# Windowed attention and a feed-forward layer in float32: chunk 0's second to fourth pair of heads in split form, and a PSUM bank for each head's values

## The chip, the cores and the metric

One core of a Trainium2 chip runs the whole program. The metric is the time of one execution on the device, in microseconds (us). The kernel before took 1069.58 us, the median of three runs (1069.06 to 1069.76). One further execution was taken with the hardware profiler; every row of a trace in this text is from such a profiled execution.

Engines are named as the profile does: PE is TensorE (matmul) and PEld its weight loads, DVE is VectorE, ACT is ScalarE, POOL is GpSimd, SP is SyncE, which here only issues transfers.

## The reference

The kernel computes attention over a causal window of 128 positions with a linear bias for each head, and then a two-layer feed-forward network:

```python
# q, k, v: (8, 8, 576, 64) float32
scores = scale * np.matmul(q, k.transpose(0, 1, 3, 2))
bias = slopes[:, None, None] * (-np.abs(rel))[None]       # slopes 2**-1 ... 2**-8
mask = (rel >= 0) & (rel < 128)                           # rel = row - column
scores = np.where(mask, scores + bias[None], -1e9)
attn = softmax(scores)
x = (attn @ v).transpose(0, 2, 1, 3).reshape(4608, 512)
h = x @ w_in                                              # (4608, 2048)
g = np.where(h >= 1, h, np.where(h <= -1, 0, (h + 1)**2 / 4))
out = g @ w_out                                           # (4608, 512)
```

The weights w_in and w_out arrive as float64 and are turned into float32 on the chip.

## The kernel before, in words

The 4608 tokens are cut into 12 chunks of 384 (three query blocks of 128). Within a chunk the 8 heads are taken as 4 pairs; pair p = 4c + g is pair g of chunk c, and m = 2p or 2p + 1 numbers its heads through the whole program. So heads 0 to 7 belong to chunk 0, and their pairs are 0 to 3. The feed-forward layer of a chunk needs the outputs of all its 8 heads: column block g of its input, `xn`, comes from pair g.

A head passes through these steps, each in a function of its own: `load_qk` and `load_v` start the transfers on the SP queue. `prepare_q`, `prepare_k` and `prepare_v` bring q, k and v into the form for TensorE. `scores` makes the scores (tile s), their biased maxima on DVE (line 249), the exponentials on ACT (line 251), the sum and its reciprocal (257, 258), and folds two neighbouring blocks into weights `ep` (262, 264). `weights_t` transposes `ep` (line 273, tile p), and ACT and POOL make from it the masked weights `lu`. `values` multiplies these with v (tile x) into `xn`.

There are two forms. In the **plain** form (chunks 0 and 1, `LIGHT = 2`) the operands stay in float32: one scale of q on ACT, nothing for k and v, one copy and two masks of 128x384 for `lu` (lines 276 to 279), float32 matmuls (lines 243 and 314). In the **split** form (all later chunks) each operand is a high and a low part in fp32r: q by two ACT and two DVE instructions (198, 199), k by a cast of both heads' rows and a subtraction (208, 209), v the same way (217, 218), `lu` by a cast, a subtraction and two masks of 128x768 (283 to 288), fp32r matmuls over high and low parts (245, 246, 338), and a sum of the parts for `xn` (339 to 342). For the split form the keys are loaded twice, once into each half of the partitions (lines 174 to 176).

The feed-forward layer of chunk c has 16 tiles fc of the hidden layer. `split_x` splits `xn` (xh on ACT, line 356, xl on DVE, line 357). `layer1` adds 12 fp32r matmuls into tile h (lines 363 to 365) and forms g; `layer2` follows two tiles behind and accumulates into three PSUM banks, `acc`. In chunk 0 it multiplies in float32 with `wf` (line 393), later in split form (lines 396 to 398). The weights of tile fc are fetched over the ACT queue and converted on ACT and DVE (lines 113 to 116, 135, 136), the first four in the opening of the program between the heads of chunk 0, the others beside chunk 0's own feed-forward layer.

PSUM has eight banks: three of `ps_acc` (tag acc), one for h, four that scores, transposes and values share (`bank`). In chunk 0 the two heads of a pair write the upper and lower half of one bank of `ps_acc`, and one copy of 128 rows takes both to `xn` (line 319, on ACT for g = 0 and 2, on DVE for g = 1 and 3).

SBUF tiles with one buffer set an order of their own: a tile of a tag can be written when the tile before it under this tag has been read for the last time. A plain pair with an odd number keeps k under the tag kk and v under the tag vs, tags that only the split form fills otherwise; so two plain pairs in a row have tiles of their own.

The order of each engine's instructions comes from a scheduler that moves them ahead of time by its own estimate; on the chip each engine works its list from front to back.

Of the kernel before, what the change touches and what calls it, by code (L numbers as in the profile page):

```python
# [18 lines left out]
def windowed_attention_then_ffn(  # L19
# [38 lines left out]
    NEG = -1.0e30  # L58

    LIGHT = 2  # L60
# [102 lines left out]
    def load_qk(p):  # L163

        c, g = divmod(p, NPAIR)
        n = CH + before(c) * P
        st = pair[p] = {}
        qr = st["qr"] = ap1.tile([P, CH], F32, name=f"qr_{p}", tag="qr")
        DMA.dma_start(qr, q[g * P:(g + 1) * P, c * CH:(c + 1) * CH])
        kr = st["kr"] = ap1.tile([P, 2, CH + P], F32, name=f"kr_{p}", tag="kk" if c < LIGHT and p % 2 else "kr")  # L170
        if c < LIGHT:
            DMA.dma_start(kr[:, 0, :n], k[g * P:(g + 1) * P, (c + 1) * CH - n:(c + 1) * CH])
            return
        for half in (slice(0, D), slice(D, P)):
            DMA.dma_start(kr[half, :, :n],
                          k[g * P:(g + 1) * P, (c + 1) * CH - n:(c + 1) * CH].rearrange("(j d) t -> d j t", j=2))

    def load_v(p):
        c, g = divmod(p, NPAIR)
        nb = NQB + before(c)  # L180
        if c < LIGHT and p % 2:
            t = ap1.tile([P, 2, NQB + 1, 2, D], F32, name=f"vn_{p}", tag="vs")[:, 0]
        else:
            t = ap1.tile([P, NQB + 1, 2, D], F32, name=f"vn_{p}", tag="vn")
        pair[p]["vn"] = t
        DMA.dma_start(t[:, :nb].rearrange("p i j d -> p i (j d)"),
                      v[(c + 1) * CH - nb * P:(c + 1) * CH, g * P:(g + 1) * P].rearrange("(i p) d -> p i d", p=P))

    def prepare_q(p):
        ql = pair[p]["ql"] = ap1.tile([P, 2, CH], F32R, name=f"ql_{p}", tag="ql")  # L190
        qr = pair[p]["qr"]
        if p // NPAIR < LIGHT:
# [8 lines left out]
    def prepare_k(p):  # L201
        if p // NPAIR < LIGHT:
# [8 lines left out]
    def prepare_v(p):  # L211
        if p // NPAIR < LIGHT:
# [7 lines left out]
    def scores(m, blks):  # L220
# [14 lines left out]
        for n, i in enumerate(blks):  # L235
# [5 lines left out]
            if c < LIGHT:  # L241
# [25 lines left out]
    def weights_t(m):  # L267
# [6 lines left out]
        if m < LIGHT * H:  # L274
# [17 lines left out]
    def values(m):  # L292
# [6 lines left out]
        if c == 0:  # L299

            if j == 0:
                pair[p]["px"] = ps_acc.tile([P, DM], F32, name=f"x_{m}", tag="acc")
            pb = pair[p]["px"]
        else:
            pb = bank(f"x_{m}")
        px, pf = pb[:, :CH], pb.rearrange("r (i w) -> r i w", w=P)
        o = xn[c, g][lo_rows[j]]
        if c < LIGHT:
            po = px[lo_rows[j]] if c == 0 else px[:D]
# [7 lines left out]
            if c == 0:  # L317
                if j:
                    (V.tensor_copy if g % 2 else S.copy)(xn[c, g], px)
            elif j:  # L320
# [205 lines left out]
```

## Time and profile before

| What | Value |
|---|---|
| Median of three runs | 1069.58 us |
| The profiled execution | 1071.97 us, its span 1070.3 us |
| Busy in the span: PE, PEld | 1034.4 us (97%), 900.9 us (84%) |
| Busy in the span: DVE, ACT, POOL | 790.2 us (74%), 619.1 us (58%), 370.6 us (35%) |
| Granted TensorE clock over the span | 0.99 |

A busy TensorE isn't TensorE at its peak: matmuls overlap, and their ends are modelled. So the share of 97% says little of a stretch; what one waits for there says more. A group of instructions has one row: line, engine, operation, out<-in, shape and count, then busy time and the mean of one in ns, then the idle time of the engine just ahead of them and what ended it. A row of the waits names the waiting engine, tile and line, then whom it waited for, then total, count and longest. The views by stage give the busy time of each engine in a stretch (with the number of instructions), the granted clock, the DMA share and GB/s.

### The profile page before, as it was taken

Reading aid. Unit: us, or ns where it says so; the run is one execution under the profiler, and the core shown is the slowest. Engines: PE = TensorE matmul, PEld = TensorE weight load, DVE = VectorE, ACT = ScalarE, POOL = GpSimd, SP = SyncE. Lnnn points to the kernel's source line nnn. Section 1 sums busy time; section 2 is a strip of 40 time slices with the busy share of each in tenths; the row PEclk is TensorE's granted clock in tenths of the full one; section 3 lists DMA queues with packets and bytes.
Section 4 is the critical chain, followed back from the end, with each engine's and each line's share of the span. In section 5 each row is a group of like instructions: output and inputs, shape, how many; then the busy total and the mean of one; then the engine's idle time right before and its main releaser. Section 6 shows DMA issues by size and latency. Waiting matters only on the chain.

```text
span 1070.3 us, 16779 instructions
## 1 busy us (share of the span) xinstructions
PE 1034.4 (97%) x5472; PEld 900.9 (84%) x5472; DVE 790.2 (74%) x2249; ACT 619.1 (58%) x1475; POOL 370.6 (35%) x419
## 2 busy tenths in 40 slices
PE   6899999999999999999999999999999999999998
PEld 3566667998988988998998989899899889899996
DVE  3687799888887688877678887767787897862322
ACT  4686876556655556556557556555565665742322
POOL 2121003334443343443343443443334444332221
PEclk9889999999999999999999999999999999999999
DMA  5455512121122122121211212111121221200000
GB/s 190 139 188 189 175 45 69 34 59 60 45 65 67 39 62 79 33 56 35 66 47 50 82 47 65 63 30 37 60 65 37 77 65 38 76 1 1 30 1 30
DMA packets 58903, 69.50 MB, mean 65 GB/s; under 512 B 4032, under 2 KB 44480, under 8 KB 58816
## 3 DMA queue, kind: packets, MB, share of 16 engines
q1 hardware_dynamic: 48064, 51.66, 16.8%
q10 hardware_dynamic: 10752, 16.78, 4.5%
q8 instruction: 43, 0.70, 0.3%
q14 instruction: 44, 0.36, 0.1%
HBM read 58.98 MB, written 9.44 MB: 64 GB/s over the span
## 4 chain that ended last, share of the span: by engine, by line
PE 82%; DVE 8%; ACT 5%; issue 2%; POOL 2%; DMA 0%; ACTq 0%; DVEq 0%; POOLq 0%
PE h L363 11%; PE h L364 11%; PE h L365 11%; PE acc L396 10%; PE acc L397 10%; PE acc L398 10%; PE x L338 5%; PE acc L393 3%; PE p L273 3%; PE s L246 2%; PE s L245 2%; PE x L314 2%; PE s L243 2%; ACT z L251 1%; POOL lu L288 1%
## 5 line engine op out<-in xcount | busy, mean ns | idle before, releaser
L382 POOL TENSOR_TENSOR gl<-g,gh 128x384 fp32r<-128x384 f32 x176 | 184.1, 1046 | 434.9 <-ACT gh L381 422.0
L363 PE MATMUL h<-xh,wi 128*128 128x384 f32 x768 | 265.0, 345 | 1.8 <-ACT sg L372 1.6
L364 PE MATMUL h<-xl,wi 128*128 128x384 f32 x768 | 260.3, 339 | 0.6 <-DVE xl L357 0.6
L365 PE MATMUL h<-xh,wi 128*128 128x384 f32 x768 | 259.4, 338 | 0.0
L396 PE MATMUL acc<-wo,gh 128*128 128x512 f32 x528 | 211.8, 401 | 8.1 <-ACT gh L381 8.1
L373 DVE SCALAR_TENSOR_TENSOR g<-sg 128x384 f32<-128x384 f32 x192 | 108.6, 565 | 150.4 <-ACT sg L372 139.0
L397 PE MATMUL acc<-wo,gh 128*128 128x512 f32 x528 | 207.8, 394 | 0.0
L381 ACT CAST gh<-g 128x384 fp32r<-128x384 f32 x176 | 90.4, 513 | 192.5 <-DVE g L374 182.1
L372 ACT ACTIVATE sg<-h,quarter 128x384 f32<-128x384 f32 x192 | 111.2, 579 | 141.4 <-PE h L365 140.6
L251 ACT ACTIVATE z<-z,nmax 128x256 f32<-128x256 f32 (+2 forms) x288 | 139.2, 486 | 33.8 <-DVE nmax L249 31.7
L398 PE MATMUL acc<-wo,gl 128*128 128x512 f32 x528 | 155.5, 398 | 0.0
L363 PEld LDWEIGHTS h<-xh,wi 128*128 128x128 f32 x768 | 144.5, 188 | 11.0 <-ACT sg L372 3.2
L364 PEld LDWEIGHTS h<-xl,wi 128*128 128x128 f32 x768 | 144.5, 188 | 7.2 <-issue 2.0
L365 PEld LDWEIGHTS h<-xh,wi 128*128 128x128 f32 x768 | 144.4, 188 | 0.0
L249 DVE CUSTOM_DVE_ANT_0 z<-s,rel 128x256 f32<-128x256 f32 (+2 forms) x256 | 94.3, 394 | 52.8 <-PE s L246 43.3
L264 DVE CUSTOM_DVE_ANT_0 ep<-z,rc 128x128 f32<-128x128 f32 x256 | 129.4, 546 | 1.5
L286 POOL TENSOR_SCALAR_AFFINE_SELECT lu<-lu 128x768 fp32r<-128x768 f32 x80 | 80.7, 1008 | 128.7 <-DVE lu L284 120.1
L396 PEld LDWEIGHTS acc<-wo,gh 128*128 128x128 f32 x528 | 99.4, 188 | 27.3 <-ACT gh L381 10.5
L374 DVE SCALAR_TENSOR_TENSOR g<-sg,g 128x384 f32<-128x384 f32 x192 | 111.9, 583 | 3.7
L398 PEld LDWEIGHTS acc<-wo,gl 128*128 128x128 f32 x528 | 97.0, 188 | 19.7 <-POOL gl L382 0.2
L397 PEld LDWEIGHTS acc<-wo,gh 128*128 128x128 f32 x528 | 99.4, 188 | 16.5
L288 POOL TENSOR_SCALAR_AFFINE_SELECT lu<-lu 128x768 fp32r<-128x768 f32 x80 | 81.3, 1017 | 4.6
(78 smaller groups left out, 1451.4 us busy)
## 6 DMA issues: line engine op xcount, KB each, us to landing
kr<-in_k_dram SPq DMA_DIRECT2D x60, 256.0 KB, 3.8
qr<-in_q_dram SPq DMA_DIRECT2D x48, 192.0 KB, 3.4
out_dram<-o SPq DMA_DIRECT2D x36, 256.0 KB, 2.3
rawi<-in_moe_w_in_dram ACTq DMA_DIRECT2D x16, 512.0 KB, 3.9
rawo<-in_moe_w_out_dram ACTq DMA_DIRECT2D x16, 512.0 KB, 5.0
vn<-in_v_dram SPq DMA_DIRECT2D x32, 256.0 KB, 2.7
kr<-in_k_dram SPq DMA_DIRECT2D x28, 192.0 KB, 3.2
vn<-in_v_dram SPq DMA_DIRECT2D x16, 192.0 KB, 2.5
```

The costliest lines, as they stand in the source:

```text
L251: S.activation(z[:, i, c0:], z[:, i, c0:], AF.Exp, bias=nmax[:, i:i + 1], scale=-1.0, accum_out=sm[:, i, 0:1])
L264: st["folded"] = V.tensor_tensor_reduce(out=ep[:, i, :], in0=z[:, i, :P], in1=z[:, i, P:], op0=ALU.add, op1=ALU.add, scale=rc[:, i:i + 1], ...
L363: T.matmul(ph, wi[fc][:, 0, cc, :], xh, start=(cc == 0), stop=False)
L364: T.matmul(ph, wi[fc][:, 0, cc, :], xl, start=False, stop=False)
L365: T.matmul(ph, wi[fc][:, 1, cc, :], xh, start=False, stop=(cc == NCC - 1))
L372: first = S.activation(sg, ph, AF.Relu, bias=quarter[:, 0:1], scale=0.25)
L373: V.scalar_tensor_tensor(g, sg, 0.5, sg, ALU.min, ALU.mult)
L374: last = V.scalar_tensor_tensor(g, sg, -0.25, g, ALU.add, ALU.max)
L382: G.tensor_tensor(gl, g, gh.bitcast(F32), ALU.subtract)
L396: T.matmul(a, gh[:, ts], wo[fc][:, 0], start=first, stop=False)
L397: T.matmul(a, gh[:, ts], wo[fc][:, 1], start=False, stop=False)
L398: T.matmul(a, gl[:, ts], wo[fc][:, 0], start=False, stop=last)
```

## The change

`LIGHT` goes. A function `plain(p)` says for each pair whether it is plain: pair 0, and the four pairs of chunk 1. Pairs 1 to 3 of chunk 0 are now in split form. In `values` every head of chunk 0 gets a bank of `ps_acc` for itself, and `xn` is filled head by head: for the two heads of pair 0 by a DVE and an ACT copy of 64 rows, for heads 2 to 7 by the sum of the split form.

```diff
-    LIGHT = 2
+    def plain(p):
+
+        return p == 0 or NPAIR <= p < 2 * NPAIR
...
-        kr = st["kr"] = ap1.tile([P, 2, CH + P], F32, name=f"kr_{p}", tag="kk" if c < LIGHT and p % 2 else "kr")
-        if c < LIGHT:
+        kr = st["kr"] = ap1.tile([P, 2, CH + P], F32, name=f"kr_{p}", tag="kk" if plain(p) and p % 2 else "kr")
+        if plain(p):
...
-        if c < LIGHT and p % 2:
+        if plain(p) and p % 2:
             t = ap1.tile([P, 2, NQB + 1, 2, D], F32, name=f"vn_{p}", tag="vs")[:, 0]
...
-        if m < LIGHT * H:
+        if plain(m // 2):
             own = lu[:, 0, 1::2, :].bitcast(F32)
...
-        if c == 0:
-
-            if j == 0:
-                pair[p]["px"] = ps_acc.tile([P, DM], F32, name=f"x_{m}", tag="acc")
-            pb = pair[p]["px"]
-        else:
-            pb = bank(f"x_{m}")
+
+        pb = ps_acc.tile([P, DM], F32, name=f"x_{m}", tag="acc") if c == 0 else bank(f"x_{m}")
         px, pf = pb[:, :CH], pb.rearrange("r (i w) -> r i w", w=P)
         o = xn[c, g][lo_rows[j]]
-        if c < LIGHT:
-            po = px[lo_rows[j]] if c == 0 else px[:D]
+        if plain(p):
+            po = px[:D]
...
-            if c == 0:
-                if j:
-                    (V.tensor_copy if g % 2 else S.copy)(xn[c, g], px)
-            elif j:
+            if j:
                 S.copy(o, po)
             else:
                 V.tensor_copy(o, po)
```

The same replacement of `c < LIGHT` by `plain(p)` stands in `prepare_q`, `prepare_k`, `prepare_v` and `scores`. Lines behind `plain` move by two, those behind `values` by minus six.

The scheduler puts the new instructions between the old ones. In the rows below a tile's name is followed by the number of its pair (kr, kk, kl, vn, vs, ql) or head (s, z, rc, ep, p, lu, x) and a running number.

On DVE, in the opening, from the maxima of head 3 to the sum of its exponentials; before:

```order
L249 ISA z_3_235,nmax_3_236<-s_3_2_244,rel_98 128x256
L249 ISA nmax_3_236 128x1
L115 TENSOR_SCALAR f_i0_221<-rawi0_125 128x512
L116 ISA f_i0_221<-rawi0_125,f_i0_221 128x1024
L257 TENSOR_REDUCE rc_3_248<-sums_108 128x3
L258 RECIPROCAL rc_3_248<-rc_3_248 128x3
L262 TENSOR_TENSOR ep_3_234<-z_3_235,rc_3_248 128x128
```

And after the change:

```order
L251 ISA z_3_248,nmax_3_249<-s_3_2_259,rel_98 128x256
L251 ISA nmax_3_249 128x1
L201 SCALAR_TENSOR_TENSOR ql_2_274<-qr_2_183,ql_2_274 64x384
L138 TENSOR_TENSOR wi0_238<-f_i0_233,wi0_238 128x512
L220 TENSOR_TENSOR vs_1_316<-vn_1_196,vs_1_316 128x6x64
L286 TENSOR_TENSOR lu_2_284<-p_2_285,lu_2_284 128x3x128
L117 TENSOR_SCALAR f_o0_294<-rawo0_128 128x512
L259 TENSOR_REDUCE rc_3_264<-sums_108 128x3
```

The low parts of pair 2's q, of pair 1's v and of head 2's weights stand ahead of head 3's sum. With heads 2, 4, 6 and 7 only one or two instructions stand at this place.

On SP, from the third transfer on, before:

```order
L186 DMA vn_0_117<-in_v_dram 128x3x128
L172 DMA kr_1_123<-in_k_dram 128x384
L169 DMA qr_1_121<-in_q_dram 128x384
L186 DMA vn_1_187<-in_v_dram 128x3x128
L172 DMA kr_2_177<-in_k_dram 128x384
L169 DMA qr_2_175<-in_q_dram 128x384
```

And after:

```order
L188 DMA vn_0_117<-in_v_dram 128x3x128
L171 DMA qr_1_121<-in_q_dram 128x384
L177 DMA kr_1_123<-in_k_dram 64x2x384 x2
L171 DMA qr_2_183<-in_q_dram 128x384
L177 DMA kr_2_185<-in_k_dram 64x2x384 x2
L188 DMA vn_1_196<-in_v_dram 128x3x128
L177 DMA kr_3_281<-in_k_dram 64x2x384 x2
```

The keys come in two transfers of half the partitions. Pair 1's v (vn_1) has moved behind the keys of pair 2, and its tile is now that of pair 0's v, which the values of head 1 read last.

On PE, from the end of the first hidden tile (h_0_0) on, before:

```order
L363 MATMUL h_0_0_600<-xh_0_3_596,wi0_226 128x384
L273 MATMUL p_9_571<-ident_82,ep_9_508 128x128
L364 MATMUL h_0_0_600<-xl_0_3_597,wi0_226 128x384
L365 MATMUL h_0_0_600<-xh_0_3_596,wi0_226 128x384
L314 MATMUL x_8_637<-lu_8_535,vn_4_454 64x256 x2
L314 MATMUL x_8_637<-lu_8_535,vn_4_454 64x128 x2
L243 MATMUL s_11_0_646<-kr_5_440,ql_5_529 128x256 x2
L243 MATMUL s_11_2_653<-kr_5_440,ql_5_529 128x192
L273 MATMUL p_10_707<-ident_82,ep_10_549 128x128 x3
L363 MATMUL h_0_1_664<-xh_0_0_584,wi1_283 128x384
```

And after:

```order
L357 MATMUL h_0_0_689<-xh_0_3_685,wi0_238 128x384
L275 MATMUL p_9_660<-ident_82,ep_9_592 128x128
L311 MATMUL x_8_726<-lu_8_619,vn_4_532 64x256 x2
L311 MATMUL x_8_726<-lu_8_619,vn_4_532 64x128 x2
L275 MATMUL p_9_660<-ident_82,ep_9_592 128x128 x2
L358 MATMUL h_0_0_689<-xl_0_3_686,wi0_238 128x384
L359 MATMUL h_0_0_689<-xh_0_3_685,wi0_238 128x384
L245 MATMUL s_11_0_735<-kr_5_509,ql_5_613 128x256 x2
L245 MATMUL s_11_2_742<-kr_5_509,ql_5_613 128x192
L275 MATMUL p_10_796<-ident_82,ep_10_638 128x128 x3
L311 MATMUL x_9_839<-lu_9_659,vn_4_532 64x256 x2
```

The values of head 8 have moved ahead of the end of the first hidden tile, and those of head 9 ahead of the second. From the fifth hidden tile of chunk 0 on the lists of PE are the same in both kernels, and those of the other engines from about there.

More of the change, by code (lines that the diff above doesn't have):

```diff
@@ L191, in prepare_q @@
         qr = pair[p]["qr"]
-        if p // NPAIR < LIGHT:
+        if plain(p):
             S.activation(ql[:, 0].bitcast(F32), qr, AF.Copy, scale=qscale[:, p % NPAIR:p % NPAIR + 1])
@@ L201, in prepare_k @@
     def prepare_k(p):
-        if p // NPAIR < LIGHT:
+        if plain(p):
             return
@@ L211, in prepare_v @@
     def prepare_v(p):
-        if p // NPAIR < LIGHT:
+        if plain(p):
             return
@@ L240, in scores @@
             win.append((o, c0, lone))
-            if c < LIGHT:
+            if plain(p):
                 r, qs, ks = lo_rows[j], slice(i * P, (i + 1) * P), slice(k0, k0 + 2 * P - c0)
@@ L298, in values @@
             xn[c, g] = xp1.tile([P, CH], F32, name=f"xn_{c}_{g}", tag=f"xn{g}")
-        if c == 0:
-            if j == 0:
-                pair[p]["px"] = ps_acc.tile([P, DM], F32, name=f"x_{m}", tag="acc")
-            pb = pair[p]["px"]
-        else:
-            pb = bank(f"x_{m}")
+        pb = ps_acc.tile([P, DM], F32, name=f"x_{m}", tag="acc") if c == 0 else bank(f"x_{m}")
         px, pf = pb[:, :CH], pb.rearrange("r (i w) -> r i w", w=P)
         o = xn[c, g][lo_rows[j]]
-        if c < LIGHT:
-            po = px[lo_rows[j]] if c == 0 else px[:D]
+        if plain(p):
+            po = px[:D]
             todo = [i for i in (0, 1, 2, -1) if i + b0 >= 0]
```

## The prediction

> **What bounds the kernel now.** I read the chain of waits first, then a table by stage of the stretch that it points to. In the chain the change can only touch the opening of the program; from the first accumulating matmul of the second layer (line 393) on, TensorE runs without a gap.
>
> ```profile
> 34.05 2.33 PE x L314 x6
> 36.38 2.43 PE s L243 x6
> 38.81 2.32 PE x L314 x6
> ...
> 44.97 1.30 PE x L314 x6
> ...
> 51.45 1.34 ACT z L251 x5
> 52.79 0.19 ACT z L251
> 53.01 0.17 DVE rc L257
> 53.20 0.19 DVE rc L258
> ...
> 62.36 2.75 PE x L314 x8
> 65.11 1.95 PE s L243 x6
> 67.07 0.48 PE p L273 x3
> 67.55 0.18 PE h L363
> ...
> 69.66 1.44 PE x L314 x8
> 71.11 0.63 PE acc L393
> ```
>
> The columns are start, duration, engine, tile, line. Two things are to be seen. The float32 score (s) and value (x) matmuls of chunk 0 lie on the chain, at 2.3 to 2.4 us a head in one place and 1.30 us in another, so TensorE's clock was not the same. And the last stretch, from 62.36 to 71.11, is a queue of TensorE alone.
>
> ```profile
> core 0: us, PE busy (x) PEld busy (x) DVE busy (x) ACT busy (x) POOL busy (x), PEclk, DMA share, GB/s
> 12.30:61.30 49.00, 43.20 (x139) 24.87 (x139) 30.90 (x139) 31.71 (x90) 10.21 (x21) 0.84 0.45 145
> 61.30:71.10 9.80, 9.80 (x42) 7.00 (x40) 8.54 (x30) 8.42 (x21) 2.43 (x5) 0.75 0.42 136
> ```
>
> I cut the opening where VectorE stands at the same work in both kernels: at 12.3 it has finished the maxima of head 1, and at 61.3 it has finished xl of the fourth column block (line 357), which the first hidden tile (fc 0) needs last. In those 49.0 us VectorE is busy 30.90 and idle 18.1. Its three largest waits tell why:
>
> ```profile
> DVE rc L257 <- ACT z L251: 10.4, 6, 4.3
> DVE z L249 <- PE s L243: 3.8, 3, 3.0
> DVE xn L319 <- PE x L314: 2.2, 2, 1.1
> ```
>
> 6.0 of it are waits for TensorE directly, 10.4 for the exponentials, which themselves were late behind TensorE in part. So the opening is paced by TensorE and by the round of one head (scores, maximum, exponential, fold, transpose, mask, values), with VectorE in reserve.
>
> **What the change takes from TensorE.** A plain head has 640 score columns and 640 value columns in float32. The split head has 1280 of each in fp32r. From a later chunk:
>
> ```profile
> 183.95 0.82 PE x L338 x7
> ```
>
> Seven split value matmuls take 0.82, five take 0.59, against 1.30 at full clock for the plain head; the scores, with as many columns, go the same way. That is about 1.4 us a head at full clock and 2.4 at half, for six heads 8.5 to 14.5 us of TensorE. If TensorE alone paced the opening, all of it would be won.
>
> **What it adds.** These rows give the mean of each added form over the whole kernel (after the bar: busy, mean ns):
>
> ```profile
> L199 DVE SCALAR_TENSOR_TENSOR ql<-qr,ql 64x384 fp32r<-64x384 f32 x80 | 59.3, 742 | 2.6 <-ACT ql L198 0.2
> L209 DVE TENSOR_TENSOR kl<-kr,kk 128x768 fp32r<-128x768 f32 x12 | 13.6, 1135 | 0.1
> L218 DVE TENSOR_TENSOR vs<-vn,vs 128x384 fp32r<-128x384 f32 x12 | 6.9, 573 | 0.0
> L284 DVE TENSOR_TENSOR lu<-p,lu 128x384 fp32r<-128x384 f32 x80 | 44.4, 555 | 4.6 <-ACT lu L283 3.3
> L340 DVE TENSOR_TENSOR xn<-x,xn 64x384 f32<-64x384 f32 x80 | 43.7, 546 | 4.1 <-ACT xn L339 2.9
> L342 DVE TENSOR_TENSOR xn<-x,xn 64x128 f32<-64x128 f32 x80 | 22.3, 279 | 1.8
> L319 DVE COPY xn<-x 128x384 f32<-128x384 f32 x2 | 1.1, 558 | 2.2 <-PE x L314 2.2
> ```
>
> A pair costs VectorE 2x0.742 (ql) + 1.135 (kl) + 0.573 (vs) + 2x0.555 (lu) + 2x0.546 + 2x0.279 (xn) = 5.95 us. Three pairs are 17.9. One of their old copies (g = 1) and that of g = 3 go, 2x0.558, and pair 0 gains a copy of 64 rows, taken as long as one of 128: together 17.3. The window has its own level for a form that both have:
>
> ```profile
> L264 DVE CUSTOM_DVE_ANT_0 ep<-z,rc 128x128 f32<-128x128 f32 x20 | 6.4, 363 | 0.1
> L264 DVE CUSTOM_DVE_ANT_0 ep<-z,rc 128x128 f32<-128x128 f32 x256 | 129.4, 546 | 1.5
> L286 POOL TENSOR_SCALAR_AFFINE_SELECT lu<-lu 128x768 fp32r<-128x768 f32 x80 | 80.7, 1008 | 128.7 <-DVE lu L284 120.1 <-DVE rc L257 8.5
> ```
>
> The fold takes 363 ns in the window and 546 in the whole kernel, a ratio of 0.66, so the lower bound of the added work is 0.66 x 17.3 = 11.4 us and the upper one 17.3. GpSimd's share explains the difference: 10.21 of 49.0 now; with twelve selects of 1.0 us in place of twelve of half that it comes to about 16 of 49, near the page's 35% for the whole kernel. I take 15.5, nearer to the upper end. The Trainium skill, "SBUF — State Buffer", on what shares the port pair, says that a VectorE instruction with two SBUF inputs and a GpSimd instruction that reads SBUF lock each other out; the rise from 363 to 546 agrees, and by that rule alone the sum would take the 17.3.
>
> ScalarE gains a kk and a vs cast, a second half of ql, and copies of 64 rows instead of 128:
>
> ```profile
> L193 ACT ACTIVATE ql<-qr,qscale 128x384 f32<-128x384 f32 x8 | 4.8, 604 | 1.1 <-PE s L243 1.1
> L198 ACT ACTIVATE ql<-qr 64x384 fp32r<-64x384 f32 x80 | 41.7, 521 | 1.0
> L208 ACT CAST kk<-kr 128x768 fp32r<-128x768 f32 x12 | 10.0, 836 | 1.6 <-PE s L245 1.4
> L217 ACT CAST vs<-vn 128x384 fp32r<-128x384 f32 x12 | 6.1, 512 | 1.6 <-PE x L338 1.6
> L339 ACT COPY xn<-x 64x384 f32<-64x384 f32 x80 | 38.1, 476 | 16.0 <-PE x L338 12.7 <-DVE xl L357 1.8
> ```
>
> With ql at 0.60 now and 2x0.52 then, a pair is 0.44 + 0.84 + 0.51 + about 0.7 = 2.5 us, three pairs 7.5; 31.7 + 7.5 = 39.2 of 49 leaves room, but ScalarE is in order and its casts now stand between exponentials. The keys are loaded twice (two DMAs of 64 partitions, 590 KB more over three pairs) at a DMA share of 0.45: I cost the bytes at nothing, hidden by the gaps between transfers, 1 us if not. The bank for each head costs nothing: the eight tiles of chunk 0 are read before the accumulators ask for the banks, with the queue from 62.36 to 71.11 in between.
>
> **What stays idle.** VectorE after: 30.9 + 15.5 = 46.4 us of work in a stretch of 49.0. It would be no later only if 2.6 of the 18.1 idle us stayed. In the order shown above I count the places where nothing stands between a head's maxima and its sum to cover the exponentials (1.34 + 0.19, that is 1.5 us): heads 2, 4, 6 and 7 have one or two instructions there, and 0.6 to 1.0 us stay at each, 3.4 in all. Head 2's scores stand behind the kl of pair 1 and the float32 values of head 0, still at half clock: 1.6 us. The values of pair 1 lose the tile of their own:
>
> ```profile
> vn<-in_v_dram SPq DMA_DIRECT2D x4, 192.0 KB, 5.3
> ```
>
> Their load now starts when head 1's value matmuls are done and takes 5.3 us; the cast vs of pair 1 waits for it, and queued behind that cast on ScalarE stand lu of head 2, a weight conversion and the exponentials of head 3, for which VectorE waits: 2.0 us. The new copies on ScalarE before each xn sum: 0.5. I keep 7.5 us; the bounds are 0 and 18.1. **So xl of the fourth block ends at 30.9 + 15.5 + 7.5 - 49.0 = 4.9 us later.**
>
> **From there to line 393's first matmul.** Now 1.06 us remain of the first hidden tile, then come x of head 8 (2.75), s of head 11 (1.95), p of head 10 (0.48), the second hidden tile (67.55 to 69.66, 2.11) and x of head 9 (1.44): 9.8 us. Afterwards head 8's values stand ahead of the first tile's end, where TensorE waits anyway: 2.75 go. The maxima of head 10 stand behind xl on VectorE in both:
>
> ```profile
> L249 DVE CUSTOM_DVE_ANT_0 z<-s,rel 128x256 f32<-128x256 f32 x192 | 76.2, 419 | 35.2 <-PE s L246 32.6 <-PE s L243 1.5
> ```
>
> Three maxima (1.26), the exponentials (1.5), the sum and its reciprocal (0.4), a copy that stands there afterwards (0.56) and a fold (0.36) make 4.1, against 3.0 of TensorE work (1.06 + 1.95), so p of head 10 is 1.1 late.
>
> ```profile
> 32.30:42.30 10.00, 9.47 (x25) 0.50 0.43 147
> ```
>
> Here TensorE is busy 9.47 of 10.0 us with plain matmuls, and the granted clock stays at 0.50. The Trainium skill, "TensorE: Matmul & The Clock Gate", part 1, puts the return to full clock after one busy window of about 3.4 us; this stretch disagrees, so the row decides: a busy queue of ten microseconds can stay at half clock. After the change TensorE is idle more in the opening, so I expect the half clock as far as the second hidden tile: 2.11 more (nothing if the clock is full by then, and some 7 us if another ten of the same queue run at half). Tail: -2.75 + 1.1 + 2.1 = +0.45.
>
> **The sum** is 4.9 + 0.45, about **+5.3 us**. Behind line 393's first matmul both orders hold the same work and are identical from the fifth hidden tile on, so the shift stays. The profiled execution took 1071.97 us (span 1070.3), which becomes 1077.3; it was 2.4 above the median of the runs, 1069.58, on whose scale the forecast is **1074.9**.
>
> **Rivals.** (1) **Faster**: the new work falls into VectorE's waits, 2 us stay idle, the added work costs 11.4 to 14, and the clock is full for the second tile: 30.9 + 14 + 2 - 49 = -2.1, with the tail at -2.75: about 1064.7. It decides from the point where less than 2.6 us stay idle. For it speaks that 6.0 us of the waits are for TensorE, which has half the work; against it the in-order ScalarE. Chance 0.13. (2) **Absorbed**: TensorE has waits of its own later, at the passage to chunk 1:
>
> ```profile
> 150.00:190.00 40.00, 36.41 (x185) 29.09 (x184) 37.77 (x101) 27.21 (x65) 13.27 (x12) 1.00 0.22 63
> ```
>
> 3.6 us idle there, beside a VectorE busy 37.77 of 40. A VectorE that caught up before would take the shift out: 5.3 - 3.6 = 1.7, 1071.3, within 0.2%. Against it: its order is fixed and its work there waits for what TensorE sends. Chance 0.20. (3) **Worse**: ScalarE becomes the bound through the late vs, or the half clock lasts through the first accumulations: +10, 1079.6. Chance 0.12. That the form is not taken up is no case: the instructions of the order are those of later chunks.
>
> **How the numbers follow.** The forecast, from +2.1 to +9, has 0.55. A measurement of this kernel tells about 0.2%, 2.1 us, from no change. Slower is 0.55 + 0.12 = 0.67, within 0.2% is 0.20, faster 0.13. The range from 1067.0 to 1082.0 holds the forecast, the absorbed case, most of the worse one and the edge of the faster one; what is left out is about 0.2.
>
> **What would show it.** In the changed profile: VectorE busy about 46 us from the maxima of head 1 to the fourth xl, which ends near 66; a wait of the vs cast for the load vn; line 393's counterpart starting near 76; the clock at 0.50 up to about 70. Wrong if that matmul starts before 71 (rival 1), or starts late while the end does not move (rival 2).

## The result and the profile after

| | before | after |
|---|---|---|
| Median of the first comparison (4 runs each) | 1069.67 us | 1081.35 us |
| Median of a later comparison (11 and 6 runs) | 1069.19 us | 1081.25 us |
| Profiled execution, its span | 1071.97, 1070.3 us | 1081.9, 1079.7 us |
| Start of the first accumulating matmul | 71.11 us | 78.99 us |
| End of xl of the fourth block | 61.3 us | 70.1 us |

The change makes the kernel slower: the ratio is 1.0104 (95% interval 1.0084 to 1.0124) in the first comparison and 1.0113 (1.0093 to 1.0134) in the second. The forecast was 1074.9 us. In all comparisons of this study together, 118 runs of before have a median of 1071.6 and quartiles of 1069.3 and 1073.3; ten runs of after have 1081.3. Executions that the profiler shows at a much lower granted clock (two of before, of 1131 and 1673 us, and one of the variant dve_act_apart, of 1156.55) are left out of every median here. On that broader base the change costs 9.7 us. Each later comparison ran on a chip of its own, with medians of before from 1069.2 to 1072.6; whether the chip makes that difference or chance does was not tried, so the cost lies between 9.7 and 12.1 us.

The first view is the table by stage of after, cut at the same work as in the prediction: from the end of the maxima of head 1 (now 12.6) to the end of the fourth xl, and from there to the first accumulating matmul.

```profile
core 0: us, PE busy (x) PEld busy (x) DVE busy (x) ACT busy (x) POOL busy (x), PEclk, DMA share, GB/s
12.60:70.10 57.50, 38.13 (x133) 27.68 (x134) 48.88 (x169) 39.12 (x104) 15.93 (x21) 0.67 0.45 138
70.10:79.00 8.90, 8.90 (x42) 6.74 (x41) 7.54 (x30) 7.47 (x18) 1.42 (x3) 0.84 0.50 169
```

The stretch has grown from 49.0 to 57.5 us. TensorE is busy 38.13 of it, less than the 43.20 of before although its clock was 0.67 and not 0.84, so it has 19 us to spare; it isn't off the chain of waits, though, which passes through it several times between 52.7 and 65 us. VectorE has gone from 30.90 busy to 48.88, and its idle time from 18.1 to 8.6. ScalarE has gone from 31.71 to 39.12, GpSimd from 10.21 to 15.93.

Next, the waits of VectorE in this stretch of after:

```profile
DVE lu L286 <- ACT lu L285: 1.7, 2, 0.9
DVE rc L259 <- ACT z L253: 1.7, 5, 0.7
DVE z L251 <- PE s L248: 1.1, 1, 1.1
DVE xn L334 <- ACT xn L333: 1.0, 1, 1.0
DVE f_i L117 <- ACT rawi L115: 0.8, 1, 0.8
DVE xn L317 <- PE x L311: 0.7, 1, 0.7
```

The wait for exponentials has shrunk from 10.4 us to 1.7 and those for TensorE from 6.0 to 1.8. Two new ones, 1.7 and 1.0, are the split form's own: a subtraction or a sum on VectorE waits for the cast or copy on ScalarE just ahead of it. No row names a load.

The groups of VectorE in the same stretch of after show what the work consists of:

```profile
L266 DVE CUSTOM_DVE_ANT_0 ep<-z,rc 128x128 f32<-128x128 f32 x20 | 7.4, 409 | 0.0
...
L286 DVE TENSOR_TENSOR lu<-p,lu 128x384 fp32r<-128x384 f32 x6 | 3.3, 554 | 1.8 <-ACT lu L285 1.7
L201 DVE SCALAR_TENSOR_TENSOR ql<-qr,ql 64x384 fp32r<-64x384 f32 x6 | 3.3, 553 | 0.2
L334 DVE TENSOR_TENSOR xn<-x,xn 64x384 f32<-64x384 f32 x6 | 3.3, 548 | 1.2 <-ACT xn L333 1.0
L118 DVE CUSTOM_DVE_ANT_0 wf<-rawo,f_o 128x1024 uint16<-128x1024 uint16 x3 | 3.0, 1012 | 0.1
L211 DVE TENSOR_TENSOR kl<-kr,kk 128x768 fp32r<-128x768 f32 x3 | 2.9, 951 | 0.0
...
L220 DVE TENSOR_TENSOR vs<-vn,vs 128x384 fp32r<-128x384 f32 x3 | 2.2, 744 | 0.0
...
L336 DVE TENSOR_TENSOR xn<-x,xn 64x128 f32<-64x128 f32 x6 | 1.7, 281 | 0.2
```

The six added forms sum to 3.3 + 3.3 + 3.3 + 2.9 + 2.2 + 1.7 = 16.7 us; one copy of 0.55 less makes it 16.1. The rise of VectorE's busy time is 18.0. The rest, 1.9, is in instructions that both kernels have: the fold `ep` takes 409 ns where before took 363 (7.4 against 6.4 us), and `wf` 1012 where before had 685 (3.0 against 2.1 us). Four smaller groups nearly cancel: the two on line 117 take 0.6 us more each, `wi` 0.4 and the plain sum for `ep` on line 264 0.5 less.

Where the longer folds lie is seen in the timeline of after: a fold with GpSimd at rest, then two later ones, then GpSimd in the same two microseconds (start, duration, engine):

```profile
45.41 0.35 DVE L266 CUSTOM_DVE_ANT_0 ep<-z,rc 128x128 f32<-128x128 f32 x1
...
50.10 0.96 DVE L266 CUSTOM_DVE_ANT_0 ep<-z,rc 128x128 f32<-128x128 f32 x1
...
50.99 1.00 DVE L266 CUSTOM_DVE_ANT_0 ep<-z,rc 128x128 f32<-128x128 f32 x1
...
50.05 0.86 POOL L288 TENSOR_SCALAR_AFFINE_SELECT lu<-lu 128x768 fp32r<-128x768 f32 x1 [5.61 <-DVE lu L286]
50.98 0.87 POOL L290 TENSOR_SCALAR_AFFINE_SELECT lu<-lu 128x768 fp32r<-128x768 f32 x1
```

The first takes 0.35 us. Each of the two others begins within 0.05 us of a mask, lasts 0.10 to 0.13 us longer than the mask, and so nearly three times as long as the first. The Trainium skill, "SBUF — State Buffer", section "Who interferes with whom", says that a VectorE instruction with two SBUF inputs contends with a GpSimd instruction that reads SBUF, and that the one that issues second is blocked until the first is done; these rows agree with it.

Last, the chain of waits of after. First a piece of the opening, then the queue behind the fourth xl:

```profile
32.90 1.07 ACT z L253 x5
...
34.90 0.48 ACT lu L285
35.38 0.56 ACT rawo L115
35.95 0.57 ACT rawo L116
36.52 0.13 ACT kk L210
...
40.86 0.55 DVE ql L201
...
41.45 0.56 DVE lu L286
...
43.80 1.06 DVE vs L220
...
69.65 2.75 PE x L311 x8
72.40 0.62 PE p L275 x2
73.02 0.18 PE h L358
73.20 0.17 PE h L359
73.37 1.38 PE s L245 x6
74.76 0.48 PE p L275 x3
75.24 1.45 PE x L311 x8
...
78.99 1.29 PE acc L387 x3
```

From 33 to 46 us the chain runs through ScalarE and VectorE, where the one of before ran through TensorE's x and s up to 43. The queue behind the fourth xl has no gap, and takes 8.9 us where it took 9.8.

### The profile page after: what moved, and what is told of

The parts are those of the page before. It is cut to its first block, busy times and chain, and to the rows that moved or that the text cites. A ratio compares the mean times of both kernels' runs of the same rounds, so it can differ in the third digit from the quotient of the medians.

```text
span 1079.7 us, 16821 instructions
## 1 busy us (share of the span) xinstructions
PE 1030.2 (95%) x5466; PEld 905.0 (84%) x5466; DVE 807.7 (75%) x2278; ACT 627.2 (58%) x1489; POOL 373.8 (35%) x419
## 4 chain that ended last, share of the span: by engine, by line
PE 81%; DVE 8%; ACT 5%; issue 2%; POOL 2%; DMA 1%; ACTq 0%; DVEq 0%; POOLq 0%
PE h L357 11%; PE h L358 11%; PE h L359 11%; PE acc L390 10%; PE acc L391 10%; PE acc L392 10%; PE x L332 5%; PE acc L387 3%; PE p L275 3%; PE s L247 2%; PE s L248 2%; PE x L311 1%; ACT z L253 1%; POOL lu L290 1%; PE s L245 1%
## 5 line engine op out<-in xcount | busy, mean ns | idle before, releaser
L288 POOL TENSOR_SCALAR_AFFINE_SELECT lu<-lu 128x768 fp32r<-128x768 f32 x86 | 86.5, 1006 | 159.6 <-DVE lu L286 150.9
L390 PEld LDWEIGHTS acc<-wo,gh 128*128 128x128 f32 x528 | 99.3, 188 | 27.3 <-ACT gh L375 10.5
L332 PEld LDWEIGHTS x<-lu,vs 128*128 128x128 f32 x542 | 77.3, 196 | 20.2 <-POOL lu L290 16.0
```

Source lines behind the costliest of these rows:

```text
L332: T.matmul(ox, w, lx, start=(n == 0), stop=(n == len(todo) - 1), skip_group_check=True)
L390: T.matmul(a, gh[:, ts], wo[fc][:, 0], start=first, stop=False)
```

## The experiments

Three theories were set against each other. **V**: the change's added work on VectorE paces the opening. **T**: TensorE, and its half clock above all, still paces it. **L**: loads that wait for shared tiles do. "A" in an edit is the changed kernel, "B" the one before. The last column is the ratio less one, times 1071.6.

| Run | Edit in a few words | median (runs) | ratio to before (95%) | us by the ratio |
|---|---|---|---|---|
| bank_alone | A, all chunk 0 plain | 1073.04 (10) | 1.0007 (0.9988 to 1.0025) | +0.8 |
| split_p3 | A, pair 3 alone split | 1073.28 (10) | 1.0016 (1.0003 to 1.0030) | +1.7 |
| split_p23 | A, pairs 2 and 3 split | 1076.31 (6) | 1.0052 (1.0030 to 1.0074) | +5.6 |
| split_p1 | A, pair 1 alone split | 1070.82 (10) | 0.9989 (0.9971 to 1.0008) | -1.2 |
| pe_more | A, more score matmuls | 1084.22 (4) | 1.0106 (1.0081 to 1.0132) | +11.4 |
| no_low | A, no low part of the weights | 1075.51 (10) | 1.0035 (1.0018 to 1.0053) | +3.8 |
| hi_only | A, high parts alone | 1070.98 (10) | 1.0003 (0.9981 to 1.0025) | +0.3 |
| scores_split | A, values plain | 1074.81 (12) | 1.0032 (1.0016 to 1.0048) | +3.4 |
| dve_more | B, more VectorE work | 1080.32 (5) | 1.0063 (1.0033 to 1.0092) | +6.8 |
| pe_cheap | B, less TensorE work | 1067.14 (10) | 0.9958 (0.9943 to 0.9972) | -4.5 |
| pool_more | B, masks twice | 1071.51 (10) | 0.9994 (0.9972 to 1.0016) | -0.6 |
| act_more | B, more ScalarE work | 1073.29 (12) | 1.0024 (1.0007 to 1.0040) | +2.6 |
| dve_act | B, both of these | 1083.45 (6) | 1.0128 (1.0108 to 1.0149) | +13.7 |
| rebuilt | dve_act, less TensorE work | 1077.62 (6) | 1.0070 (1.0053 to 1.0087) | +7.5 |
| rebuilt_pool | rebuilt, masks twice | 1078.35 (6) | 1.0079 (1.0061 to 1.0096) | +8.5 |
| after_again | the changed kernel | 1081.25 (6) | 1.0113 (1.0093 to 1.0134) | +12.1 |
| dve_act_apart | dve_act, ScalarE writes elsewhere | 1082.61 (4) | 1.0098 (1.0080 to 1.0115) | +10.5 |
| rebuilt_apart | rebuilt, ScalarE writes elsewhere | 1077.41 (6) | 1.0047 (1.0032 to 1.0063) | +5.0 |

Before itself had medians of 1069.2 to 1072.6 in these comparisons, so a ratio carries some 2 us of that. It isn't the quotient of two medians either: by medians dve_more is 9.5 us over before and act_more 4.1. Where two experiments are compared with each other, I use their medians, which carry the same scatter.

### The parts of the change

**bank_alone**: the bank for each head, all of chunk 0 plain.

```diff
-        return p == 0 or NPAIR <= p < 2 * NPAIR
+        return p < 2 * NPAIR
```

> All four pairs of chunk 0 plain as before; of the change only the PSUM bank for each head's values stays, with its copies of 64 rows (two more on VectorE, two more on ScalarE than before). Theory V (VectorE paces the opening after the change): 1 us more VectorE work in 18 us of idle time, so 1069 to 1071 us. Rival T (TensorE's half clock paces it) and rival L (loads that wait for shared tiles) say the same: nothing. If this part had a price of its own it would show here as 1073 or more.

No cost can be told from nothing: the interval holds 1. (The time is a little over the 1073 named ahead, but before had 1071.73 beside it.) The costed zero of the bank stands, within some 2.7 us.

**split_p1**, **split_p3** and **split_p23**: pair 1 alone, pair 3 alone, or pairs 2 and 3 in split form.

```diff
-        return p == 0 or NPAIR <= p < 2 * NPAIR
+        return p != 1 and p < 2 * NPAIR                 # split_p1
+        return p < 3 or NPAIR <= p < 2 * NPAIR          # split_p3
+        return p < 2 or NPAIR <= p < 2 * NPAIR          # split_p23
```

> Pair 1 alone in split form, the one whose k and v wait for the tiles of pair 0. V: as for pair 3 alone, +0 to +3 us over 1069.6. T: about +4. L: most of the change's +11.7, +6 or more.

> Pair 3 alone in split form. V: 6 us more VectorE work, which VectorE's 18 idle us before xl of the fourth column block mostly take up, so +0 to +3 us over 1069.6. T: a third of the change, about +4. L: pair 3 has no plain neighbour behind it whose tile it waits for that the whole change doesn't have too, so about 0.

> Pairs 2 and 3 in split form. V: 12 us more VectorE work; the idle time is nearly used up, +3 to +7 us over 1069.6, and the third pair then costs more than the first. T: two thirds, about +8. L: little, below +3, since pair 1 with its late loads is plain.

One pair costs from -1.2 to +1.7 us, two cost 5.6, three (the change) 11 to 12 by the comparisons beside it: each further pair costs more than the one before it. The table by stage of split_p1, up to the end of its fourth xl, tells why one is nearly free:

```profile
12.40:59.50 47.10, 36.97 (x142) 22.92 (x142) 38.79 (x151) 34.81 (x97) 13.68 (x21) 0.82 0.51 162
```

VectorE's added work has gone into its waits here: 38.79 busy and 8.3 idle, in a stretch that is no longer than before's 49.0. (This profiled execution, 1067.76 us, was the fastest of the ten, so the length itself says little.) With 8.3 us idle, near the 8.6 that are left after the whole change, I take its reserve to be used up there, and what comes on top to lengthen the stretch. The other profiles bear this out: VectorE is busy 38.67 of 49.3 us in split_p3, 43.54 of 52.8 in split_p23, 42.87 of 52.0 in no_low (below) and 48.72 of 57.2 in a second profile of the change. In all of them the stretch is VectorE's work and 8 to 11 us of idle time. Pair 1 is also the one whose v loses its tile, so theory L, which needed a loss here, falls.

### Taking work out of the changed kernel

**no_low** leaves out the low part of the weights of heads 2 to 7 (subtraction, half of each mask, its matmuls); **hi_only** leaves out all low parts of these heads.

```diff
+        if m < H:                                       # no_low, hi_only
+            ga = S.copy(lu[:, 0, 1::2, :], pt)
...
+            done_t[m] = [ga.ins, gg.ins]
+            return
...
+            if p < NPAIR:                               # hi_only
+                S.mul(ql[lo_rows[j], j], qr[lo_rows[j]], 2.0 ** (2 * (p % NPAIR) + j + 1) / 8.0)
+                continue
```

> The changed kernel without the low part of the softmax weights in heads 2 to 7 of chunk 0 (that part of the product is left out): per head one VectorE subtraction and one short sum less, GpSimd's masks of 384 in place of 768 columns, two value matmuls less. V: VectorE has 3.3 + 1.7 us less and GpSimd 6 us less to collide with: 1074 to 1077. T: TensorE's queue is thinner still, no gain, 1080 to 1083.

> Heads 2 to 7 of chunk 0 with the high parts alone, in fp32r (all low parts of q, k, v and the weights are left out): TensorE's saving and more, almost no VectorE work beside the plain form. V: the opening is no longer paced by TensorE nor by VectorE's added work: 1064 to 1069. T: TensorE is idle most of the opening and at half clock longer: 1072 or more.

no_low came out as V had it: without six subtractions of 0.55 us and six short sums of 0.28, with half the masks and two value matmuls a head less, it is 5.8 us faster than the change by the medians (1075.51 against 1081.26). hi_only missed V's range at its upper end. Its table by stage and VectorE's waits say why:

```profile
12.30:60.90 48.60, 37.73 (x111) 22.81 (x111) 34.81 (x148) 39.03 (x106) 11.16 (x23) 1.00 0.52 165
```

```profile
DVE rc L270 <- ACT z L264: 6.8, 7, 2.1
DVE f_o L117 <- ACT rawo L115: 4.2, 3, 1.8
```

With VectorE at 34.81 and the clock at 1.00 all along, VectorE waits 6.8 and 4.2 us for ScalarE, which is the busiest engine with 39.03. So V alone was too narrow, and ScalarE is a second load. T expected a longer half clock here, and it was full.

**scores_split** keeps the split scores of pairs 1 to 3, and makes weights and values plain.

```diff
-        if plain(m // 2):
+        if plain_v(m // 2):          # p < 2 * NPAIR; the same in load_v, prepare_v, values
```

> Pairs 1 to 3 of chunk 0 with the scores in split form and the values plain: 6 us more VectorE work and 4 us more ScalarE work, for half of TensorE's saving, and no more GpSimd work. V: VectorE's idle time takes the work up as with one split pair, and TensorE's saving pays about as much: 1068 to 1072 against some 1071.5 of before. T: about +5, 1076.

At 1074.81 it lies between the two expectations, 1072 and 1076. VectorE is busy 37.89 us of the 49.2 up to its fourth xl, and ScalarE 35.30:

```profile
12.40:61.60 49.20, 37.16 (x136) 23.89 (x136) 37.89 (x142) 35.30 (x94) 10.09 (x18) 0.79 0.51 154
```

**pe_more** gives TensorE more work than the change took from it: four matmuls more ahead of each group of split scores, whose results are overwritten.

```diff
+            if c == 0:
+                for _ in range(4):
+                    T.matmul(o, ql[:, j, i * P:(i + 1) * P], kk[:, j, k0:k0 + 2 * P - c0], start=True, stop=True)
```

> The changed kernel, with four further score matmuls ahead of each split one in heads 2 to 7 (overwritten by the real ones): a head's columns on TensorE are again what a plain head has. V: TensorE has 19 us idle in the opening, so the time stays near the changed kernel's 1081, 1080 to 1084. T, if TensorE's time counts there: +8 us, 1089. T, if the half clock is the cause: the fuller queue lifts the clock sooner, 1075 to 1078.

```profile
12.40:73.00 60.60, 47.56 (x205) 38.06 (x206) 49.05 (x169) 39.15 (x105) 15.91 (x21) 0.76 0.41 132
```

The time, 1084.22, is at V's upper end and far from both of T's. TensorE is busy 47.56 us up to the fourth xl, 9.4 more than in the change, and by the medians that costs 3 us. So inside the change about a third of added TensorE time counts.

### Putting single parts into the kernel before

**dve_more** adds five subtractions in each of heads 2 to 7, **act_more** three copies, **pool_more** two masks; all write a part of `lu` that nobody reads there.

```diff
             ga = S.copy(own, pt)
+            if 2 <= m < H:
+                scr = lu[:, 1, 1::2, :].bitcast(F32)
+                for _ in range(5):                      # dve_more
+                    V.tensor_tensor(scr, pt, own, ALU.subtract)
+                for _ in range(3):                      # act_more
+                    S.copy(scr, pt)
+                low = lu[:, 1, 0::2, :].bitcast(F32)    # pool_more
+                G.affine_select(out=low, in_=own, pattern=[[0, NQB], [-1, P]],
...
```

**pe_cheap** takes work from TensorE: the upper halves of the operands as bfloat16, the lower halves left out.

```diff
+                if 1 <= p < NPAIR:
+                    T.matmul(o, ql[r, 0, qs].bitcast(BF16)[:, 1::2], kr[r, 0, ks].bitcast(BF16)[:, 1::2], start=True, stop=True)
+                    continue
```

> The kernel before, with five subtractions of 128x384 on VectorE added in each of heads 2 to 7, whose results nothing reads: 16.5 us more VectorE work, TensorE, ScalarE, GpSimd and the loads as before. V: 1076 to 1081 against some 1071.7 of before. T and L: below 1073.

> Kernel before, with three more ScalarE copies of 128x384 in each of heads 2 to 7 of chunk 0, behind the copy of the weights; their results are read by nobody. Eighteen copies by 0.467 us (line 276 in the opening of before) are 8.4 us of ScalarE work, about as much as the 7.5 us that the prediction counted for the change and called room. If ScalarE's added work is a second part of the slowdown (theory V with ScalarE: VectorE's work +9, ScalarE's +4, TensorE's saving -4.5), the fourth xl ends 3 to 5 us later than in before and the time is 3 to 5 us above the runs of before beside it. If ScalarE has room, as the prediction had it, the shift is 0 to 1.5 us, and VectorE's work alone stands against TensorE's saving. If ScalarE is as tight as VectorE, it is 7 to 9 us.

> The kernel before, with GpSimd's two masks taken twice in heads 2 to 7 (6 us of GpSimd work more, results unread): GpSimd's part of the change alone. V: the masks lie between transpose and values, and GpSimd collides with VectorE somewhat more: 1072 to 1075, a minor part of the change's cost. If contention were the main cost: 1077 or more.

> The kernel before, with the upper halves of the float32 words (as bfloat16) as operands of the score and value matmuls of heads 2 to 7: TensorE takes one pass in place of four there, and nothing is added on any other engine (the lower halves are left out of the products). It prices TensorE's saving by itself, against some 1071.5 us of before. V: the saving ends the waits for TensorE (6 us of VectorE's idle time directly), and then ScalarE and VectorE pace: 1066 to 1069. T: the thinner queue keeps TensorE at half clock and the saving is lost: 1071 or more.

The table by stage of dve_more, and the granted clock of pe_cheap from 28 to 58 us:

```profile
12.40:71.20 58.80, 50.09 (x147) 29.55 (x147) 46.06 (x175) 32.93 (x94) 10.80 (x21) 0.83 0.37 121
```

```profile
28.00:58.00 30.00, 24.94 (x72) 0.51 0.44 141
```

VectorE's added work, in a kernel that is otherwise the one before, stretches the opening to 58.8 us, more than the change's 57.5. It isn't a pure addition of work, though. The subtractions read the part of `lu` that GpSimd's second mask overwrites, so this mask waits for all five of them, where the change has one subtraction ahead of its masks. The waits of GpSimd in the same stretch of dve_more show it:

```profile
POOL lu L283 <- DVE lu L280: 12.2, 6, 4.5
```

In before no mask waits for VectorE. So a part of what dve_more costs is a longer round of each head, and no run separates the two; the same holds for the kernels below that are built on it.

TensorE's relief alone makes the kernel 4.5 us faster, and it does so with a clock of 0.51 for thirty microseconds: with dve_more, T falls twice. ScalarE's copies cost 2.6 us (0.7 to 4.3), less than expected and more than room would. Doubled masks cost nothing that can be measured where VectorE has idle time. The profiled execution of act_more took 1070.54 us, though its median is 1073.29, and that of pool_more 1079.6 with a median of 1071.51: the opening of one kernel differs by some microseconds from execution to execution, so I read sizes from the medians and only kinds from a profile.

### The parts together

**dve_act** has both additions, **rebuilt** also pe_cheap's operands with each matmul issued twice, **rebuilt_pool** also the masks; in **dve_act_apart** and **rebuilt_apart** ScalarE's copies write another part of the tile than VectorE's subtractions.

```diff
+                    for _ in range(2):                  # rebuilt: scores, and values alike
+                        T.matmul(o, ql[r, 0, qs].bitcast(BF16)[:, 1::2], kr[r, 0, ks].bitcast(BF16)[:, 1::2], start=True, stop=True)
...
-                    S.copy(scr, pt)                     # the two apart
+                    S.copy(lu[:, 1, 0::2, :].bitcast(F32), pt)
```

> The changed kernel itself once more, beside more runs of before, since its first time (+11.7 us by medians) stands on four runs each, and the runs of before have since scattered from 1068 to 1075. If the opening's shift at the first accumulating matmul (+7.9 us in the profile) is all of it, the difference of the medians is 7 to 10 us. If something behind the opening adds to it each time, it is 10.5 to 13.5 us.

> Kernel before, with the five VectorE subtractions of dve_more and the three ScalarE copies of act_more in each of heads 2 to 7. One at a time they gave ratios of 1.0063 (+6.8 us) and 1.0024 (+2.6 us). If the parts simply add (theory V with ScalarE), this is +8 to +11 us. If the two engines pass a head back and forth, so that each lengthens the other's waits, it is +12 to +18. If VectorE alone sets the pace, +6 to +8.

> dve_act, and the score and value matmuls of heads 2 to 7 with the upper halves of their operands in bfloat16, each matmul issued twice, so that TensorE has 1280 columns of one pass a head for each, as in the split form. It leaves out the lower halves, and the values of these heads are twice as large. So before gets the change's added work on VectorE (16.5 us) and ScalarE (8.4 us) and its saving on TensorE, without its tiles, loads and masks. If these three terms are what the change does to the opening, the time is as in after_again, within 2 us of it. If it stays under +5 us over before, something else that the change brings (its masks of twice the size, its loads, its order) carries the rest.

> rebuilt, and in heads 2 to 7 GpSimd's two masks a second time, on another part of the tile, so that GpSimd's work on the weights is that of the change (two masks of 128x768). The output is that of rebuilt. If GpSimd's masks slow the VectorE instructions beside them, as the profile of the change suggests for the fold (409 ns against 363) and wf (1012 against 685), this is 1.5 to 4 us slower than rebuilt. If GpSimd's masks cost nothing here, as pool_more says for a VectorE with idle time, the two are the same within 1 us.

The table by stage of rebuilt, then the fold's group in rebuilt_pool:

```profile
12.40:67.60 55.20, 41.46 (x142) 24.37 (x143) 47.03 (x175) 41.24 (x112) 11.18 (x22) 0.63 0.39 128
```

```profile
L269 DVE CUSTOM_DVE_ANT_0 ep<-z,rc 128x128 f32<-128x128 f32 x20 | 7.8, 422 | 0.0
```

dve_act cost 13.7 us by its ratio, in the range of two engines that lengthen each other's waits; but by medians its 14.3 are about the sum of 9.5 and 4.1, so that they do is not shown. rebuilt met neither of its two expectations: it stayed 3.6 us short of the change, and 8.4 over before. rebuilt_pool came out as if the masks cost nothing. These three and after_again ran beside the same runs of before, so their medians compare directly: 1083.45 with the two additions, 1077.62 with TensorE's relief on top (-5.8), 1078.35 with the masks (+0.7, with the intervals of the two overlapping), 1081.25 for the change. The three terms and the masks thus make 9.2 of the 12.1 us that the change shows over before there. The fold does stretch to 422 ns with the masks, as in the change (409). The last 2.9 us come from something that the rebuilt kernel lacks: the form's own order, waits, loads and matmuls. No run separates these.

> dve_act with ScalarE's copies on another part of the tile than VectorE's subtractions. In dve_act both wrote the same part, and ScalarE waited 3.4 us there for VectorE, which the change doesn't do. If that coupling made the two parts cost more together than one by one (ratios 1.0063 and 1.0024, together 1.0128), the ratio falls to about 1.008 to 1.0095 (+8.5 to +10 us). If VectorE and ScalarE lengthen each other's waits in any case, it stays at 1.011 to 1.014.

> rebuilt with ScalarE's copies on another part of the tile than VectorE's subtractions; as in rebuilt the lower halves of the operands of heads 2 to 7 are left out and their values are twice as large. If the coupling through the shared part carried some of rebuilt's ratio of 1.0070, it falls to 1.003 to 1.0055, and more of the change's 1.0113 is then due to its own order and waits. If VectorE's work fills the opening there without it (47.0 busy of 55.2 us), the ratio stays at 1.006 to 1.008.

Both are inconclusive. Their medians are about those of the coupled kernels (1082.61 and 1077.41); the ratios fell only because the runs of before beside them had a median of 1072.3 and not 1069.2. And the wait that the edit should remove is still there in rebuilt_apart's waits of ScalarE:

```profile
ACT lu L287 <- DVE lu L285: 3.1, 3, 1.4
```

So some of rebuilt's slowdown may come from this wait, which the change doesn't have, or from the mask that waits for five subtractions. The 9.2 us are an upper bound for the terms.

## Why the prediction was right in direction and too small

The forecast of +5.3 us is about half of what was measured. Of the signs it named, VectorE's work came to 48.9 us (46 forecast), the fourth xl to 70.1 (66), the first accumulating matmul to 79.0 (76) and the end of the half clock to 72.9 (70). The wait of the vs cast for its load did not come.

**What bounds the kernel: right.** The change acts in the opening. The shift at the first accumulating matmul is 7.9 us, and it stays: no later stage takes it back, so rival 2 fell. Rival 1 needed no more than 2.6 us of VectorE's idle time to stay; 8.6 stayed.

**TensorE's saving: right in kind.** Priced through VectorE's idle time and not as a gain of its own. TensorE's busy time fell by 5.1 us and not by 8.5 to 14.5, at a lower clock. pe_cheap, which takes away more than the change does, is worth 4.5 us (3.0 to 6.1).

**The work on VectorE: the step that failed first.** The prediction's sum was "30.9 + 15.5 + 7.5 - 49.0 = 4.9"; the added work measured 18.0 in place of 15.5, above the upper bound of 17.3. The new forms themselves were bounded well (16.1 net). The other 1.9 us are in rows of both kernels, above all the longer fold and wf: the prediction used the lengthening beside GpSimd to price the added rows, and did not apply it to the rows that were there already. For the fold, rebuilt_pool shows that masks alone do it (392 ns in rebuilt, 422 with them), though its time rose by no more than 0.7 us, inside the scatter; for wf no run does.

**What stays idle: 7.5 counted, 8.6 measured, by other items.** The wait of pair 1's vs cast for its load, 2.0 us, did not occur: the cast ran at 24.86 us without a wait. The exponentials cost 1.7 in place of 3.4. Head 2's scores cost 1.1 in place of 1.6. In their place stand the waits of the split form's own pairs of instructions (1.7 and 1.0), of which the prediction had 0.5, 0.8 for a weight conversion on ScalarE and 0.7 for values. With the start of the stretch 0.3 later, the fourth xl ends 8.8 us later, where 4.9 were forecast. That the count of the idle time came near is luck: three of its four items were off by half or more. These sizes are of one profile of before and one of after; a second profile of after (57.2 us, 48.72 busy) agrees, before has no second.

**"Leaves room" for ScalarE: wrong.** The size was right (7.5 counted, 39.12 - 31.71 = 7.4 measured), but the chain runs through ScalarE, and act_more shows 2.6 us for about as much work where nothing was costed. That rival 3 (1079.6) came nearest in size is half a coincidence: it expected ScalarE as the bound through a late vs, or the half clock through the first accumulations. The vs cast wasn't late, and the clock was full from 72.9, ahead of the first accumulation at 79.0.

**The tail: 0.45 forecast, -0.9 measured, with all three terms wrong.** The sum was -2.75 + 1.1 + 2.1. The values of head 8 do stand ahead of the first hidden tile's end in the list, but TensorE came to them only at 69.65, as the fourth xl was ending: 2.3 of their 2.75 us lie behind it, and 0.45 were won. Head 10's p wasn't late: in the chain it follows the scores directly at 74.76. And the half clock did not reach the second hidden tile:

```profile
70.00:72.00 2.00, 2.00 (x8) 0.50 0.00 0
72.00:74.00 2.00, 2.00 (x9) 0.77 0.00 0
74.00:76.00 2.00, 2.00 (x11) 1.00 0.63 170
```

A mean of 0.77 between 72 and 74 puts the change to 1.00 at about 72.9, some 3.3 us after the queue of the chain begins at 69.65. So the scores of head 11 took 1.38 us in place of 1.95, which with those 0.45 makes about the 0.9, and the 2.1 us were wrongly charged. Before has a stretch that went the other way, with no idle time of TensorE in the record:

```profile
56.00:66.20 10.20, 10.20 (x29) 0.50 0.49 162
```

The Trainium skill, "TensorE: Matmul & The Clock Gate", part 1, puts the return to full clock after one busy window of about 3.4 us. The 3.3 us of after agree with it, these 10.2 us don't; what lifts the clock stays open here.

**Behind the accumulations: 0 forecast, 1.5 measured** (a span 9.4 us longer, of which 7.9 stand at the first accumulating matmul). In the changed kernel's profile one stretch of 20 us has a mean clock of 0.91. Cut finer, it is half the clock for 3.4 us, behind a lull of TensorE:

```profile
680.00:700.00 20.00, 20.00 (x103) 0.91 0.25 83
...
677.00:680.40 3.40, 1.96 (x9) 1.00 0.00 0
680.50:683.90 3.40, 3.40 (x14) 0.50 0.02 5
```

TensorE is busy all through it, so I estimate its cost at half of 3.4 us, 1.7, near the 1.5. The profile of before has no such stretch, although it has a lull of the same length (1.45 us idle between 668 and 672, at a clock of 1.00). dve_act and pe_more have one at the same place, and dve_more, no_low and act_more one between 900 and 940. So the work of the change isn't needed for it; why before's profile was spared is open.

**The base.** The forecast stood on 1069.58, the median of three runs, which lies in the lowest third of the 118 runs seen since. Against their median of 1071.6 two of the 6.4 us between forecast and result are the base, and nothing of the kernel, if that median and not the 1069.2 to 1069.7 beside the runs of after is taken. Of the rest, 3.9 are the opening (2.5 work, 1.1 idle, 0.3 start), -1.35 the tail, 1.5 the stretch behind; 0.4 are rounding and the step from profiled executions to medians.

**The bank** cost nothing that can be measured, as forecast. That the doubled loads of the keys cost nothing was not tried by itself; no wait names them.

No variant was shown to beat the kernel before. split_p1 is the nearest, at 0.9989 with an interval that holds 1. pe_cheap is faster, but leaves out the lower half of each operand.

## What to carry to other kernels

An engine with idle time takes added work for nothing only until its idle time is down to what the round of dependences leaves; here one pair of heads went into 18 us of idle VectorE nearly for nothing, the third cost more than twice the first, and 8 to 11 us stayed idle with one, two and three pairs alike. A place ahead in an engine's list is no place ahead in time: the values of head 8 moved up in TensorE's list and still ran for the most part behind the fourth xl, since a matmul ahead of them waited for xh. Moving work off a busy engine must be paid for on every engine that gets some, the second busiest included, and instructions that were there already can get longer beside the new ones. Before a forecast of half a per cent is put on a median of three runs, the scatter of the kernel itself should be known.

## What the runs showed of the hardware

- Two executions of one kernel differ by several microseconds in what seems the same work: of 118 runs of before 49 lie under 1070.5 and 47 over 1072.5, with 22 between. Their granted clocks go with it, 0.992 to 0.994 in the lower group and mostly 0.986 to 0.989 in the upper; that the clock is the cause isn't shown.
- A half clock need not hurt: pe_cheap ran at 0.51 for 30 us, with TensorE busy 24.94 of them, and is the fastest kernel of the study. Its three runs with a mean clock of 0.997 or more took 1067.7 to 1070.0 us, the other seven, at 0.982 to 0.984, 1065.8 to 1067.3.
- A fold of VectorE that takes 0.35 us by itself took 0.96 and 1.00 beside masks of 0.86 and 0.87 on GpSimd.
- TensorE's clock fell to 0.50 for 3.4 us in the changed kernel behind a lull of 1.4 us, with 1.96 of the 3.4 us before it busy. Means of 0.91 over 20 us, from 660 to 700 or from 900 to 940, stand in most profiles.
- A queue of TensorE with no idle time in the record ran at 0.50 for 10.2 us (before, 56.0 to 66.2), and another was back at full clock after 3.3 us (after, from 69.65).
